# Talking-heads attention with an FNet block: raw q and k turned by VectorE in 32x32 blocks instead of by TensorE through PSUM, from the second batch on

## The chip, the cores and the metric

The kernel runs on one core of a Trainium2 chip. The metric is the device time of one execution in microseconds, the median of several runs. All data is float32.

## The reference

```python
# q, k, v: (8, 12, 448, 64)   w_pre, w_post: (12, 12)
scores = einsum("bhij,hg->bgij", (q @ k.T) / sqrt(64), w_pre)
attn   = exp(scores - max(scores, -1)); attn /= attn.sum(-1) + 1e-9
x      = (einsum("bgij,gh->bhij", attn, w_post) @ v)      # -> (8, 448, 768)
u      = x + real(fft(fft(x, axis=1), axis=2))
un     = (u - mean(u)) / sqrt(var(u) + 1e-6)
out    = u + relu(un @ w_ch1) @ w_ch2                     # 768 -> 3072 -> 768
```

The mixing of the 12 heads before and after the softmax sets the layout of the attention stage: scores of all heads must stand side by side on partitions. The weights `w_ch1` and `w_ch2` come as float64 and are converted in the kernel.

## The kernel before

The kernel has two parts: `mix_phase` (attention and Fourier mixing, to about 800 us) and `ffn_phase`. Only the first is touched.

`mix_phase` runs 184 steps, 23 for each of 8 batches (`GS` = 23, `TOT` = 184), after a prologue with negative step numbers. In step `s` these things happen, in an order that is written out by hand in `ORDERS`, one list for even steps and one for odd:

- `pre`: TensorE mixes the scores of step s+2 over heads (L656, into PSUM tiles `mx`).
- `post`: TensorE mixes the exponentials of step s over heads (L690, into `po`).
- `max0`, `max1`: VectorE takes the row maxima of step s+2 (L663). `exp0`, `exp1`: ScalarE takes the exponentials into `PP`, with their sums (L670).
- `turn`: VectorE turns `po` of step s in 32x32 blocks into `Pv` (L703).
- `scale`: VectorE makes the reciprocal of the sums of step s+2 (L677, L678), GpSimd scales `PP` with it (L680). Behind it GpSimd does one or two pieces of the Fourier folds (L785 to L806; one if a load of q or k was issued in the step).
- `QK`, `AV`: TensorE makes scores (L628) or the product with v (L720); ScalarE evicts them (L489).
- `full`: larger pieces with due steps, among them `emit_xpose`, `emit_x`, `emit_z`, `emit_s2`.
- `conv`: VectorE does one operation of the conversion of a float64 weight (`wts.deal(1)`).
- `gather`: SP gathers the scores of step s+5 into `Kr` (L645). At the start of a step, `none` issues loads of q, k and v on GpSimd's queue.

The program order of TensorE, VectorE, ScalarE and GpSimd is the order in which the pieces are emitted, so an instruction that waits holds all that stands behind it on its engine. Each step's maxima are taken two steps before its `post`.

Raw q and k of a pair of heads (`xx` = 0, 1, 2) come by `emit_load_qk`: a tile `raw` of 128 partitions, 64 for each of two groups of heads (`y`), 7 consecutive tokens on a partition, two heads side by side (`x`), by four DMAs (L572) with 64 rows of 1792 bytes in the source, written as pieces of 256 bytes. The pool `praw` has four such tiles. `emit_xpose` turns a tile by seven 128x128 transposes on TensorE (L601) into two PSUM tiles `ms`. VectorE evicts one and ScalarE the other into `qT` or `kT` (L489), four tiles of each (`pqt`). The columns of `qT` stand in the order of the tokens; the eviction writes them in steps of 7 elements:

```python
dst = _ap(t, MG + c0, [[rt, P], [1, n], [WQ, 2], [C7, 64]])       # q
dst = _ap(t, 32 * c0, [[rt, P], [32, n], [HS, 4], [1, 32]])       # k
```

The columns of `kT` may stand in any order that agrees with the rows of v, which `emit_load_v` (L581) loads.

The due steps stand in tables, counted from the first step of the batch before: `AT_T` says at which step a tile is transposed (q and k of pair 0 at 5 and 9, of pair 1 at 15 and 16, of pair 2 at 13 and 15), `AT_L` when its two halves are loaded (-8 to -1 for the first four tiles, 8 to 11 for the last two). `AT_V` gives the steps of the v loads in their own batch, `AT_QK` those of the scores. The four `qT` tiles are used in turn, so a new one needs the last score product of the batch before (block 7) that reads the old.

## Time and profile before

| what | us |
|---|---|
| median of 3 runs | 2301.55 (2299.75 to 2306.33) |
| span of the profiled execution | 2297.6 |
| TensorE (matmul) busy | 2249.2 (98%) |
| VectorE busy | 1711.2 (74%) |
| ScalarE busy | 1167.1 (51%) |
| GpSimd busy | 1292.1 (56%) |
| granted TensorE clock, mean | 0.998 |

The span runs from the first to the last instruction of one execution that was profiled; its own time is that span. The timed runs are other executions and lie 2.2 to 8.7 us above it.

How to read the rows: PE is TensorE (PEld its weight loads), DVE is VectorE, ACT is ScalarE, POOL is GpSimd, SP the queue that issues most DMAs. A group row has line, engine, operation, out<-in, partitions x elements, count, then busy time and mean ns of one, then the idle time of the engine just before these instructions and what ended it. A timeline row has start, duration, engine, line and operation, and in brackets the idle time before it with its releaser. In the busy times by stretch, each engine has its busy us and its number of instructions, and the last three columns are clock, share of the 16 DMA engines and GB/s. A row of a DMA queue has packets, MB and the share of 16 engines' time; a row of DMA issues has their count, KB of each, and the median us from issue to landing. Matmuls are pipelined and their ends are modelled, so a busy TensorE need not be one at its peak.

### The profile page before, as it was taken

To read this page: it belongs to the slowest core of one execution; us is meant where nothing else is said; L and a number is where in the kernel's file an instruction comes from. 1 tells how busy PE (TensorE), PEld (TensorE's weight loads), DVE (VectorE), ACT (ScalarE), POOL (GpSimd) and SP (SyncE) were. 2 spreads that over 40 slices of the span, in tenths; PEclk is the share of its full clock that TensorE was granted. 3 is DMA by queue.
4 is the path that set the end of the run, shared out by engine and by line. 5 is a ranking of instruction groups with operands and counts; after the bars stand their busy time and mean duration, and the time that the engine had idled before them with its cause. 6 is when DMAs were issued, how large, how long until landed. Compare 5 with 4: busy or idle time off the path is not lost.

```text
span 2297.6 us, 60793 instructions
## 1 busy us (share of the span) xinstructions
PE 2249.2 (98%) x22894; PEld 1740.7 (76%) x22894; DVE 1711.2 (74%) x3640; ACT 1167.1 (51%) x3330; POOL 1292.1 (56%) x1805
## 2 busy tenths in 40 slices
PE   7999999999999999999999999999999999999998
PEld 3455555555554677777899999999999899999998
DVE  5778787888877757776877787778778777765545
ACT  4676767767676533231445445444444445434434
POOL 7677878879768541221555555546555645454334
PEclk9999999999999999999999999999999999999999
DMA  7566565666756475649677887788787987795664
GB/s 185 168 178 181 168 192 171 190 179 181 202 151 190 143 265 182 230 162 327 191 181 180 252 214 184 212 195 242 204 197 184 277 188 174 191 257 121 143 146 76
DMA packets 228063, 439.45 MB, mean 191 GB/s; under 512 B 35964, under 2 KB 149558, under 8 KB 227772
## 3 DMA queue, kind: packets, MB, share of 16 engines
q1 hardware_dynamic: 156620, 301.52, 38.2%
q0 software_dynamic: 68864, 133.00, 30.4%
q8 instruction: 183, 3.00, 0.6%
q10 hardware_dynamic: 2288, 1.05, 0.2%
q14 instruction: 108, 0.88, 0.1%
HBM read 213.16 MB, written 143.16 MB: 155 GB/s over the span
## 4 chain that ended last, share of the span: by engine, by line
PE 87%; DVE 5%; DMA 3%; ACT 2%; issue 1%; POOL 1%; SPq 1%; ACTq 0%; DVEq 0%; POOLq 0%
PE psP L1213 18%; PE psP L1335 14%; PE psR L1213 9%; PE psR L1335 7%; PE mx L656 6%; PE ms L720 6%; PE ms L628 5%; PE po L690 5%; PE psQ L1213 4%; PE psQ L1335 3%; PE psP L1290 3%; PE ms L845 2%; PE ms L601 2%; DMA Kr<-Sb 1%; PE psR L1290 1%
## 5 line engine op out<-in xcount | busy, mean ns | idle before, releaser
L1369 POOL DMA_DIRECT2D out_dram<-od x172 | 209.1, 1276 | 261.7 <-DVE od L1357 175.3
L680 POOL TENSOR_SCALAR PP<-PP,rcp 128x448 f32<-128x448 f32 x368 | 234.6, 647 | 170.2 <-DVE rcp L678 123.8
L670 ACT ACTIVATE PP<-mx,nmx 128x448 f32<-128x448 f32 x368 | 230.2, 631 | 165.2 <-DVE nmx L663 157.2
L663 DVE TENSOR_REDUCE nmx<-mx 128x1 f32<-128x448 f32 x368 | 212.5, 618 | 101.2 <-PE mx L656 99.1
L1176 POOL TENSOR_TENSOR hq<-h 128x128 f32<-128x128 f32 (+1 forms) x210 | 130.0, 619 | 255.9 <-ACT h L1235 122.3
L1363 ACT COPY od<-psP 128x192 f32<-128x192 f32 x488 | 156.1, 320 | 172.0 <-PE psP L1335 170.6
L1366 DVE TENSOR_TENSOR od<-od 128x768 f32<-128x768 f32 x210 | 201.3, 972 | 52.7 <-ACT od L1363 52.3
L703 DVE STREAM_TRANSPOSE Pv<-po 128x896 f32<-128x896 f32 x184 | 203.7, 1107 | 2.9 <-PE po L690 2.1
L489 ACT COPY Sb<-ms 124x448 f32<-124x448 f32 (+1 forms) x378 | 181.7, 540 | 46.0 <-PE ms L628 19.2
L656 PE MATMUL mx<-Kr,kw 60*32 60x448 f32 x2944 | 192.2, 549 | 4.3 <-ACT PP L670 2.3
L628 PE MATMUL ms<-kT,qT 64*32 64x448 f32 (+1 forms) x3072 | 191.6, 545 | 3.9 <-ACT qT L489 2.8
L720 PEld LDWEIGHTS ms<-Pv,vv 64*64 64x64 f32 x5376 | 138.1, 132 | 73.7 <-issue 48.8
L690 PE MATMUL po<-PP,kw 60*32 60x448 f32 x2944 | 184.0, 537 | 1.2 <-POOL PP L680 1.1
L1213 PE MATMUL psP<-qs,w1t 128*128 128x256 f32 x744 | 179.2, 380 | 2.4 <-DVE h L1234 1.5
L1213 PE MATMUL psP<-ks,w1t 128*128 128x256 f32 x744 | 179.3, 380 | 0.4 <-DVE h L1234 0.3
L720 PE MATMUL ms<-Pv,vv 64*64 64x120 f32 (+1 forms) x5376 | 160.8, 263 | 3.6 <-ACT Sb L489 2.2
L254 POOL TENSOR_SCALAR wst<-wst 128x256 f32<-128x256 f32 (+1 forms) x76 | 118.6, 1569 | 67.2 <-ACT wst L265 66.9
L1213 PEld LDWEIGHTS psP<-qs,w1t 128*128 128x128 f32 x744 | 139.5, 190 | 19.4 <-DVE h L1234 1.9
L1213 PEld LDWEIGHTS psP<-ks,w1t 128*128 128x128 f32 x744 | 139.5, 190 | 17.2 <-DVE h L1234 0.7
L1213 PE MATMUL psP<-ub,w1t 128*128 128x256 f32 x528 | 127.2, 379 | 1.1 <-DVE h L1234 1.1
L1234 DVE TENSOR_TENSOR h<-h,psP 128x512 f32<-128x512 f32 x42 | 28.8, 686 | 127.9 <-PE psP L1213 112.3
L1335 PE MATMUL psP<-w2t,hq 128*128 128x192 f32 x490 | 122.5, 332 | 1.2 <-DVE od L1357 1.2
(199 smaller groups left out, 5301.6 us busy)
## 6 DMA issues: line engine op xcount, KB each, us to landing
Kr<-Sb SPq DMA_DIRECT2D x730, 105.0 KB
out_dram<-od POOLq DMA_DIRECT2D x172, 384.0 KB, 6.3
qs<-ub SPq DMA_DIRECT2D x89, 384.0 KB
ks<-ub SPq DMA_DIRECT2D x88, 384.0 KB
ub<-ub SPq DMA_DIRECT2D x79, 384.0 KB
w1t<-w SPq DMA_DIRECT2D x42, 384.0 KB
w2t<-w SPq DMA_DIRECT2D x42, 384.0 KB
raw<-in_moe_w_ch_dram SPq DMA_DIRECT2D x32, 384.0 KB
```

Source lines behind the costliest of these rows:

```text
L628: nc.tensor.matmul(pss[x][o:o + hi - lo, :S], st["qT", xx][64 * x:64 * x + 64, y, lo:hi], st["kT", xx][64 * x:64 * x + 64, y, :], start=Tr ...
L656: nc.tensor.matmul(mx[x][64 * z + o:64 * z + o + 32, :S], kw1[64 * x:64 * x + KR, o:o + 32], Kr[64 * x:64 * x + KR, z, :], start=True, sto ...
L663: nc.vector.tensor_reduce(nmx[:, :], steps[T]["mx"][x][:, :S], axis=AX.X, op=ALU.max, negate=True)
L670: nc.scalar.activation(steps[T]["PP"][:, x, :], steps[T]["mx"][x][:, :S], ACTF.Exp, bias=steps[T]["nmx", x][:, :], accum_out=steps[T]["den ...
L680: nc.gpsimd.tensor_scalar(PP[:, x, :], PP[:, x, :], rcp[:, x:x + 1], 1.0, op0=ALU.mult, op1=ALU.mult)
L690: nc.tensor.matmul(po[o:o + 32, z, :S], kw2[64 * z:64 * z + KR, y, :], PP[64 * z:64 * z + KR, :, c * HS:(c + 1) * HS], start=True, stop=True)
L703: nc.vector.transpose(turned[a]["Pv"][:, j, :].rearrange("p (z s) -> p z s", z=2), steps[T]["po"][:, :, :S])
L720: nc.tensor.matmul(pss[y][64 * x:64 * x + 64, :nu * R], st["v", pr][64 * y:64 * y + 64, x, jb * D:(jb + 1) * D], _ap(Pv, 64 * y * rp + 32 ...
L1213: mm = nc.tensor.matmul(p[:, m, :], w1[i][:, kc, m * P:(m + 1) * P], ub[:, kc, :], start=i in (0, 4, 1)[:3 - seed] and m == kc == 0, stop= ...
L1335: nc.tensor.matmul(ps[j, key][:, :DQ], a, b, start=m in (0, 4), stop=True, skip_group_check=True)
L1366: eng.tensor_tensor(D[j][:, :, :], D[j][:, :, :], D[k][:, :, :], op=ALU.add)
L1369: nc.gpsimd.dma_start(out=acc[t, r, d], in_=D[j][:, :, :], accum_op=ALU.add)
```

## The change

From the second batch on, `emit_load_half` and `emit_flip` take the place of `emit_load_qk` and `emit_xpose`. The first batch stays as it was.

A half load brings one group of two heads (`y`) into a whole `raw` tile by two DMAs on GpSimd's queue, one for each head. Partition 64x + 32h + j gets the tokens 14j to 14j+13 of head x, from element 32h on: 864 consecutive floats, of which every second run of 32 is used. A flip is one VectorE transpose in 32x32 blocks, 128 partitions x 14 x 32, from this tile straight into `qT` (columns in the order of the tokens, written 14 elements apart) or `kT` (runs of 32). There are twelve loads and twelve flips to a batch where there were six tiles. The two margins of `qT` are still set to zero by GpSimd.

The flips have a place of their own in `ORDERS`, behind `turn` and ahead of `scale`. Their due steps are in `AT_F` (`AT_F1` and `AT_L1` for the first pair of the second batch), counted as before from the first step of the batch before; the order of the pairs is 0, 2, 1 (`FLIP`). v is loaded in the order that fits the new columns of `kT`, by two DMAs where there was one. At the steps 12, 13 and 15 of each batch no weight conversion is done (`BARE`), and it must be finished by the end of the stage. The last score block takes pair 2 before pair 1.

```diff
-AT_L = ((-8, -7), (-6, -5), (-4, -3), (-2, -1), (8, 9), (10, 11))
+AT_L = (-8, -7, -6, -5, 7, 8, 10, 11, 13, 13, 14, 14)
+AT_F = ((0, 1, 3, 4), (12, 12, 13, 13), (14, 15, 15, 16))
+FLIP = (0, 2, 1)
 AT_V = ((2, 3), (4, 4), (5, 6))
-AT_L1 = ((-12, -12), (-12, -12), (2, 3), (4, 5), (8, 9), (10, 11))
+AT_L1 = (-12, -12, -12, -12)
+BARE = (12, 13, 15)
+AT_F1 = (3, 4, 5, 6)
...
-         (0, 1, 2), (0, 1, 2), (0, 1, 2), (0, 1, 2))
+         (0, 1, 2), (0, 1, 2), (0, 1, 2), (0, 2, 1))
...
-    "QK max1 exp1 turn scale conv full gather",
+    "QK max1 exp1 turn flip scale conv full gather",
...
-    "AV turn exp1 scale conv gather full flush"))
+    "AV turn flip exp1 scale conv gather full flush"))
...
+    def emit_load_half(b, xx, nm, y):
+
+        t = batches[b]["raw" + nm, xx, y] = praw.tile([P, C7, 2, D], F32, name="raw" + nm,
+                                                      tag="raw")
+        src = (q if nm == "q" else k)[b, 6 * y + 2 * xx]
+        for x in range(2):
+            nc.gpsimd.dma_start(
+                out=_ap(t, 64 * x * _row(t), [[_row(t), 64], [1, FR * D - 32]]),
+                in_=_ap(src, x * S * D, [[32, 2], [FR * D, 32], [1, FR * D - 32]]))
+        return True
+
+    def emit_flip(b, xx, nm, y):
...
+        t = st[nm + "T", xx]
+        rt = _row(t)
+        if nm == "q":
+            out = _ap(t, y * WQ + MG, [[rt, P], [1, FR], [FR, 32]])
+        else:
+            out = _ap(t, y * S, [[rt, P], [32, FR], [1, 32]])
+        nc.vector.transpose(out, _ap(raw, 0, [[_row(raw), P], [D, FR], [1, 32]]))
...
+        for n in range(2):
+            nc.gpsimd.dma_start(
+                out=t[:, n, :],
+                in_=_ap(v[b, h + n], 0, [[C7 * D, 2], [FR * D, 32], [1, C7 * D]]))
...
-            for at, (a, nm, xx) in zip(AT_L if b > 1 else AT_L1, sorted(at_t, key=lambda e: e[0])):
-                for y in range(2):
-                    due("none", f + at[y] - GS if b > 1 else at[y],
-                        lambda b=b, xx=xx, nm=nm, y=y: emit_load_qk(b, xx, nm, y))
-            for xx, at in enumerate(AT_T):
-                for nm, a in zip("qk", at):
-                    due("full", f + a - GS,
-                        lambda b=b, xx=xx, nm=nm: emit_xpose(b, xx, nm))
+            for i, xx in enumerate(FLIP):
+                for j, nm in enumerate("qk"):
+                    for y in range(2):
+                        n = 4 * i + 2 * j + y
+                        at, a = AT_L[n], AT_F[i][2 * j + y]
+                        if b == 1 and i == 0:
+                            at, a = AT_L1[n], AT_F1[n]
+                        due("none", f + at - GS,
+                            lambda b=b, xx=xx, nm=nm, y=y: emit_load_half(b, xx, nm, y))
+                        due("flip", f + a - GS,
+                            lambda b=b, xx=xx, nm=nm, y=y: emit_flip(b, xx, nm, y))
...
-                    if s >= 4:
+                    if s >= 4 and (s % GS not in BARE):
                         wts.deal(1)
```

`FR` is S // 32 = 14, `D` is 64, `C7` is 7, `WQ` is the width of `qT` with its margins.

27 lines of the change are left out of this document (20 added, 7 removed).

## Prediction

> **What bounds the kernel now.** I read the page's first part, then one line's count, then the busy times by stretch.
>
> ```profile
> span 2297.6 us, 60793 instructions
> ...
> PE 2249.2 (98%) x22894; PEld 1740.7 (76%) x22894; DVE 1711.2 (74%) x3640; ACT 1167.1 (51%) x3330; POOL 1292.1 (56%) x1805
> ```
>
> ```profile
> L703 DVE STREAM_TRANSPOSE Pv<-po x184: 1094/1107/1119, 39.0 to 784.9; 128x896 f32<-128x896 f32 x184
> ```
>
> The attention stage is 184 steps (8 batches of 23), each with one L703 on VectorE: (784.9-39.0)/183 = 4.08 us a step. I take the fifth batch; its step 0 begins at 413.5 us, and its step 12, the 105th L703, at 462.4.
>
> ```profile
> core 0: us, PE busy (x) PEld busy (x) DVE busy (x) ACT busy (x) POOL busy (x), PEclk, DMA share, GB/s
> 413.50:434.00 20.50, 20.18 (x428) 11.49 (x422) 16.85 (x38) 13.61 (x46) 14.40 (x21) 1.00 0.60 191
> 434.00:462.20 28.20, 27.97 (x615) 14.21 (x599) 22.99 (x47) 21.22 (x67) 27.68 (x45) 1.00 0.71 204
> 462.20:483.60 21.40, 20.71 (x402) 11.22 (x405) 17.91 (x35) 15.79 (x46) 21.08 (x35) 1.00 0.51 159
> 483.60:491.90 8.30, 8.30 (x184) 4.63 (x168) 5.81 (x13) 5.49 (x18) 5.67 (x9) 1.00 0.76 194
> ```
>
> These are steps 0-4, 5-11, 12-16 and 17-18. TensorE is busy 97 to 100% at full clock, so it sets the time. VectorE has 21.40-17.91 = 3.5 us to spare in steps 12-16, and GpSimd, whose queue is in order, is full from step 5 to 16.
>
> **What is removed.** In each of 7 batches, six groups of seven 128x128 transposes with their evictions.
>
> ```profile
> L601 PE MATMUL ms<-ident,rawq 128*128 128x128 f32 x147 | 20.6, 280 | 4.5 <-ACT Sb L489 4.5
> L601 PE MATMUL ms<-ident,rawk 128*128 128x128 f32 x147 | 20.5, 279 | 2.4 <-ACT Sb L489 2.4
> ```
>
> ```profile
> 468.34 0.99 PE L601 MATMUL ms<-ident,rawq 128*128 128x128 f32 x7 [0.53 <-ACT Sb L489]
> 469.26 0.98 PE L656 MATMUL mx<-Kr,kw 60*32 60x448 f32 x16
> ```
>
> ```profile
> L489 DVE COPY qT<-ms 128x512 f32<-128x512 f32 x21 | 23.5, 1121 | 2.6 <-PE ms L601 2.5
> ...
> L489 DVE COPY kT<-ms 128x384 f32<-128x384 f32 x21 | 11.7, 557 | 2.8 <-PE ms L601 2.8
> ```
>
> The next group starts 0.92 us after a group of seven, so six are worth 5.5 us of TensorE a batch, 39 us in all, and 1.0 us a batch of waits for PSUM go as well ((4.5+2.4)/7; I credit 0.3 outside steps 12-16). Two groups lie in steps 5-11, four in 12-16. VectorE loses 3 x 1.121 + 3 x 0.557 = 5.0 us a batch. ScalarE's six copies count nothing: it is busy 15.79 of 21.40 and its work stays beside TensorE's.
>
> **What is added on VectorE.** Twelve block transposes ("flips") of 128x448 a batch, SBUF to SBUF, which no row shows.
>
> ```profile
> L663 DVE TENSOR_REDUCE nmx<-mx 128x1 f32<-128x448 f32 x362 | 209.0, 618 | 96.3 <-PE mx L656 94.4
> ```
>
> A key flip writes runs of 32: between half of L703 (0.55 us) and 0.62, what L663 takes for 448 elements; I take 0.61. A query flip writes single elements 56 bytes apart. The old query copy writes them 28 bytes apart and takes 1121 ns for 512, against 557 for 384 in the key copy. So 0.55 to 0.98 (448/512 x 1.12); I take 0.98, the row of the same kind.
>
> Steps 12-16 get eight flips (two queries, two keys, a query, a query and a key, a key): 4 x 0.98 + 4 x 0.61 = 6.4 us. They lose two query and two key copies (3.4 us) and, by BARE, the weight conversions of steps 12, 13 and 15: three of these rows, 1.85 us.
>
> ```profile
> 463.78 0.49 DVE L289 TENSOR_SCALAR tmp<-wst 128x384 uint32<-128x384 uint32 x1
> ...
> 468.25 0.76 DVE L293 SCALAR_TENSOR_TENSOR tmp<-raw,tmp 128x384 f32<-128x384 uint32 x1
> ...
> 472.72 0.54 DVE L297 TENSOR_TENSOR wst<-wst,tmp 128x384 f32<-128x384 f32 x1
> ```
>
> (0.49 + 0.76 + 0.60 at step 15.) VectorE's work there becomes 17.9 - 3.4 - 1.85 + 6.4 = 19.0 us, where TensorE's falls to 20.7 - 3.7 = 17.0. So VectorE is the bound there, even with no wait.
>
> **The wait that is added.** The flip of step 14 is the first of the third pair, and its two loads are issued in GpSimd's step 13. All are in order: VectorE stops in front of step 14's sums and the next maxima until both have landed; ScalarE's exponentials wait for the maxima, and TensorE for the freed PSUM. How long is there? GpSimd in steps 12 and 13 of before:
>
> ```profile
> 465.73 1.24 POOL L680 TENSOR_SCALAR PP<-PP,rcp 128x448 f32<-128x448 f32 x2
> 466.94 0.99 POOL L790 TENSOR_TENSOR xs<-xs 113x383 f32<-113x383 f32 x1
> 468.00 1.45 POOL L799 TENSOR_TENSOR xq<-xs 113x191 f32<-113x191 f32 x2
> 469.41 0.18 POOL L800 COPY xq<-xs 113x1 f32<-113x1 f32 x1
> 469.57 1.25 POOL L680 TENSOR_SCALAR PP<-PP,rcp 128x448 f32<-128x448 f32 x2
> ```
>
> ```profile
> L645 POOL DMA_DIRECT2D Kr<-Sb x6: 554/576/602, 26.0 to 28.8; - x6
> ```
>
> From the start of step 12 on VectorE: L703 1.1, two flips 2.0, the reciprocals 0.3 = 3.4; then on GpSimd the scaling 1.25, the two folds 2.65, and the first of the four issues 0.58: the second load is issued at 7.9. The flip of step 14 is reached at 2 x 4.1 + 1.1 = 9.3. So 1.4 us lie between them, and the wait is the landing time less 1.4.
>
> What is the landing time? Each load is 64 rows of 3456 bytes (216 KB, of which half is not used) against 112 KB before, and its source pattern starts with a dimension of two, where the old one started with 64. The next answers are of two stretches: 4.5 to 10 us, where the loads start with 64, and 154.8 to 157.2 us, where only the gathers into Kr move, several queued, whose source starts with ten.
>
> ```profile
> q1 hardware_dynamic: 2754, 0.68, 91.3%
> ```
>
> ```profile
> q1 hardware_dynamic: 366, 0.56, 65.3%
> ```
>
> With 64 the queue keeps 91% of the sixteen engines busy; with ten and work waiting, 65%, which is 10.4 of 16. So I take it that a transfer is spread over as many engines as its first dimension lets it, and that a load that starts with two is carried by two: 108 KB (0.1106 MB) each. The DMA answer of 400 to 600 us, and one row of the whole run:
>
> ```profile
> q0 software_dynamic: 4816, 14.50, 26.3%
> ...
> rawq<-in_q_dram POOLq DMA_DIRECT2D x30, 112.0 KB, 4.3
> vv<-in_v_dram POOLq DMA_DIRECT2D x12, 224.0 KB, 4.6
> rawk<-in_k_dram POOLq DMA_DIRECT2D x24, 112.0 KB, 5.0
> ```
>
> ```profile
> Kr<-Sb POOLq DMA_DIRECT2D x6, 105.0 KB, 3.8
> ```
>
> One engine moves 14.50/(0.263 x 16 x 200) = 0.0172 MB/us here and 0.56/(0.653 x 16 x 2.4) = 0.0223 for the gathers: 6.4 or 5.0 us for a share. Beside that a landing has a fixed part: 4.3 less 0.4 for a query's 7 KB an engine is 3.9; 3.3 by Kr, 4.6 by the keys. So 8.3 to 11.0; I take 9.6, and a wait of 8.2 us (6.9 to 9.6). If all sixteen carried it, the nearest row is vv, as large: 4.6, and a wait of 3.2.
>
> [...]
>
> Steps 12-16 then take 19.0 + 8.2, less what VectorE can carry over into steps 17-18: it has 8.30-5.81 = 2.5 us there, of which I take half (0 to 2.5), since TensorE feels the delay before. That is 26.0 against 21.4: +4.6 us a batch. The loads of step 14 follow 3.4 us behind (four issues, scaling and a fold) and VectorE works as long before it needs them, so the wait comes once. The second pair is loaded about 2.3 steps (9.4 us) before its last flip: no wait at 9.6, 1.6 us at 11.
>
> **The rest.** Steps 5-11 lose two groups: -1.84, and -0.3 of PSUM waits. Steps 0-4 get four flips, 2 x 0.98 + 2 x 0.61 = 3.2 us, into 20.50-16.85 = 3.65 us of free VectorE time: +0.5 (0 to 1.5). GpSimd issues the V loads as twelve halves instead of six; here are the scalings of steps 4 and 5, and the reader of the second:
>
> ```profile
> 434.20 1.27 POOL L680 TENSOR_SCALAR PP<-PP,rcp 128x448 f32<-128x448 f32 x2
> ...
> 440.38 0.65 POOL L680 TENSOR_SCALAR PP<-PP,rcp 128x448 f32<-128x448 f32 x1
> ```
>
> ```profile
> 441.76 0.96 PE L690 MATMUL po<-PP,kw 60*32 60x448 f32 x16
> ```
>
> The second half of that scaling ends at about 441.64, 0.1 us before TensorE reads it. Three more issues come before it in steps 4 and 5, 3 x 0.52 = 1.6 us; other batches may have slack, so +0.9 (0 to 1.6). The halved V loads (3.3 us on two engines, 7.2 in all) have four steps, 16 us, and stay hidden; the issues of q and k cost 576 ns for 723, 3.5 us a batch saved on a queue that the V halves fill again. The conversions left out at three steps are made in later ones, on VectorE time that is free; without that cover they would cost 0.5 us each.
>
> Sum: 4.6 - 1.84 - 0.3 + 0.5 + 0.9 = +3.9 us a batch, x 7 = +27 us: the profile's 2297.6 becomes 2324.6. The timed runs lie 2.2 to 8.7 us above the span; on their median, 2301.55, it is **2328.5**. By one term at a time at its end (wait -1.3 or +1.4, query flips at 0.55 -1.7, carry-over +1.2, V issues +0.7, steps 0-4 +1.0), added as independent, the case spans 2308 to 2345.
>
> **Rivals.**
> 1. *No wait, faster.* GpSimd gets ahead of VectorE, and both loads of step 13 are issued some 8 us before the flip. It decides if the gap of 1.4 us is in truth 9 us or more. Then steps 12-16 are bound by VectorE's 19.0 (-2.4), and the sum is -3.1 a batch, -22 us; if VectorE overlaps better, up to TensorE's own 39 + 7 = -46. Middle: 2268. For it: TensorE is the bound everywhere else. Against: two folds and two scalings stand before those issues. Chance 0.15.
> 2. *Sixteen engines.* Wait 3.2: steps 12-16 take 19.0 + 3.2 - 1.2 = 21.0, the sum is -1.1, -8 us: 2294. Against: the 65.3%. Chance 0.12.
> 3. *TensorE alone counts.* VectorE's lag is made up in full in later steps; then 17.0 + 8.2 - 2.5 = 22.7, +1.3, sum +0.6, +4 us: 2306. Against: L656 and L663 follow each other within a step. Chance 0.10.
> 4. *The transposes were not on the path.* TensorE's 97% hides other limits, and their removal brings nothing: +3.9 + 1.84 + 0.3 = 6.0, +42 us: 2344. Against: no other engine is over 85% outside steps 5-16. Chance 0.08.
>
> [...]
>
> **How the numbers follow.** The forecast has 0.55; 0.3% is 7 us, about what a measurement can tell from no change. Slower: forecast and rival 4, and part of 3: 0.66. Same: the rest of 3, most of 2: 0.14. Faster: rival 1 and part of 2: 0.20. The range 2280 to 2346 leaves out most of rival 1 and the top.
>
> **What would show it.** Right: the flips of the third pair's first query wait on the DMA of rawq some 8 us, seven times (about 55 us of VectorE idle), landing near 9.6 us; steps 12-16 take 26 us; query flips 0.98, key flips 0.61. Wrong: landings near 4.6, no DMA wait on VectorE, steps 12-16 under 21 us, or a step-5 scaling that costs TensorE nothing.

## The result, and the profile after

The changed kernel takes 2495.11 us (median of 4 runs, 2484.16 to 2500.30) against 2301.89 for the one before: a ratio of 1.0838, 95% interval 1.0805 to 1.0870. That is 193 us slower, where the forecast was 27 (2328.5) and the range ended at 2346. The sign was right and the size was not. The profiled execution took 2500.29, and its span is below. First the page of the changed kernel, its span and busy times, then the turns of the 184 steps (count, ns min/median/max, first and last start):

```profile
span 2498.5 us, 60298 instructions
...
PE 2301.8 (92%) x22600; PEld 1746.7 (70%) x22600; DVE 1738.2 (70%) x3682; ACT 1144.7 (46%) x3288; POOL 1318.5 (53%) x1847
```

```profile
L743 DVE STREAM_TRANSPOSE Pv<-po x184: 1081/1106/1175, 50.7 to 976.7; 128x896 f32<-128x896 f32 x184
```

The span grew by 200.9 us: TensorE stood still 148.3 us more (2498.5 - 2301.8 = 196.7, against 48.4), and was "busy" 52.6 us more with fewer matmuls. The last step starts 191.8 us later than before (976.7 for 784.9): 11.7 us are lost ahead of the first step and 180 in the steps. The other 9.1 us come behind the last step. By the starts of this row and of L703 before, the eight batches together lose 97 us in steps 12-16, 55 in steps 5-11, 18 in steps 19-22, 7 in steps 0-4 and 3 in steps 17-18. The busy times by stretch of the fifth batch, steps 0-4, 5-11, 12-16, 17-18; of the batches that turn tiles for the next, it loses most in steps 12-16 and least in 5-11:

```profile
core 0: us, PE busy (x) PEld busy (x) DVE busy (x) ACT busy (x) POOL busy (x), PEclk, DMA share, GB/s
525.99:548.05 22.06, 21.73 (x454) 12.14 (x446) 20.87 (x44) 14.38 (x48) 16.27 (x25) 1.00 0.53 158
548.05:580.19 32.14, 26.47 (x572) 13.61 (x556) 20.01 (x44) 19.28 (x63) 29.15 (x45) 1.00 0.78 170
580.19:618.44 38.25, 24.95 (x380) 11.36 (x382) 18.35 (x36) 13.44 (x42) 21.13 (x36) 0.78 0.85 163
618.44:626.90 8.46, 8.46 (x180) 4.62 (x170) 5.63 (x13) 6.00 (x19) 6.60 (x10) 0.99 0.51 120
```

Steps 12-16 take 38.25 us for 21.40; the forecast was 26.0. Steps 0-11 take 54.2 for 48.7. In steps 12-16 TensorE stands still for 13.3 us, and its granted clock is 0.78, where it was 1.00 in all four stretches of before. The flips and what they wait for (us, times):

```profile
L609 DVE STREAM_TRANSPOSE qT<-rawq x42: 899/937/1000, 60.0 to 851.7; 128x448 f32<-128x448 f32 x42
L609 DVE STREAM_TRANSPOSE kT<-rawk x42: 588/603/670, 66.5 to 856.1; 128x448 f32<-128x448 f32 x42
...
  DMA rawq<-in_q_dram: 58.3, 10
  DMA rawk<-in_k_dram: 30.1, 10
```

And the landings of the loads and of the gathers into Kr:

```profile
rawq<-in_q_dram POOLq DMA_DIRECT2D x84, 216.0 KB, 12.4
rawk<-in_k_dram POOLq DMA_DIRECT2D x84, 216.0 KB, 12.6
...
vv<-in_v_dram POOLq DMA_DIRECT2D x84, 112.0 KB, 7.2
...
Kr<-Sb POOLq DMA_DIRECT2D x6, 105.0 KB, 7.8
```

What the prediction said of the flips is there: their durations, and the wait for rawq, 58.3 us where it had about 55 (though in ten waits of up to 10.0 us). But the last row says something it had not asked: a gather into Kr, whose code did not change, lands in 7.8 us for 3.8 (six of the first, which GpSimd issues behind loads on the same queue; for SP's the trace has no landing). The waits for the gathers, of the changed kernel (us in total, times, longest; ScalarE's, then SP's own queue):

```profile
ACT Sb L494 <- DMA Kr<-Sb: 91.1, 23, 9.6
```

```profile
SPq L685 <- DMA Kr<-Sb: 162.6, 118, 6.8
```

and of the kernel before:

```profile
ACT Sb L489 <- DMA Kr<-Sb: 18.6, 9, 3.7
```

```profile
SPq L645 <- DMA Kr<-Sb: 2.6, 6, 1.1
```

### The profile page after: what moved, and what is told of

Read it like the earlier page. It is cut to its first block, busy times and chain, and to the rows that moved or that the text cites. A ratio compares the mean times of both kernels' runs of the same rounds, so it can differ in the third digit from the quotient of the medians.

```text
span 2498.5 us, 60298 instructions
## 1 busy us (share of the span) xinstructions
PE 2301.8 (92%) x22600; PEld 1746.7 (70%) x22600; DVE 1738.2 (70%) x3682; ACT 1144.7 (46%) x3288; POOL 1318.5 (53%) x1847
## 5 line engine op out<-in xcount | busy, mean ns | idle before, releaser
L696 PE MATMUL mx<-Kr,kw 60*32 60x448 f32 x2944 | 239.8, 592 | 104.9 <-ACT PP L710 74.6
L703 DVE TENSOR_REDUCE nmx<-mx 128x1 f32<-128x448 f32 x368 | 213.3, 617 | 133.0 <-PE mx L696 131.1
L730 PE MATMUL po<-PP,kw 60*32 60x448 f32 x2944 | 230.1, 590 | 28.4 <-POOL PP L720 21.8
L668 PE MATMUL ms<-kT,qT 64*32 64x448 f32 (+1 forms) x3072 | 224.9, 582 | 13.3 <-ACT Sb L494 8.9
L760 PEld LDWEIGHTS ms<-Pv,vv 64*64 64x64 f32 x5376 | 144.2, 136 | 87.0 <-issue 55.3
L696 PEld LDWEIGHTS mx<-Kr,kw 60*32 60x32 f32 x2944 | 51.8, 109 | 198.6 <-ACT PP L710 117.6
L760 PE MATMUL ms<-Pv,vv 64*64 64x120 f32 (+1 forms) x5376 | 168.0, 269 | 11.7 <-issue 6.1
L730 PEld LDWEIGHTS po<-PP,kw 60*32 60x32 f32 x2944 | 69.8, 113 | 116.5 <-issue 73.5
L668 PEld LDWEIGHTS ms<-kT,qT 64*32 64x32 f32 (+2 forms) x3072 | 68.3, 112 | 95.0 <-issue 60.6
## 6 DMA issues: line engine op xcount, KB each, us to landing
rawq<-in_q_dram POOLq DMA_DIRECT2D x84, 216.0 KB, 12.4
rawk<-in_k_dram POOLq DMA_DIRECT2D x84, 216.0 KB, 12.6
```

Source lines behind the costliest of these rows:

```text
L668: nc.tensor.matmul(pss[x][o:o + hi - lo, :S], st["qT", xx][64 * x:64 * x + 64, y, lo:hi], st["kT", xx][64 * x:64 * x + 64, y, :], start=Tr ...
L696: nc.tensor.matmul(mx[x][64 * z + o:64 * z + o + 32, :S], kw1[64 * x:64 * x + KR, o:o + 32], Kr[64 * x:64 * x + KR, z, :], start=True, sto ...
L703: nc.vector.tensor_reduce(nmx[:, :], steps[T]["mx"][x][:, :S], axis=AX.X, op=ALU.max, negate=True)
L730: nc.tensor.matmul(po[o:o + 32, z, :S], kw2[64 * z:64 * z + KR, y, :], PP[64 * z:64 * z + KR, :, c * HS:(c + 1) * HS], start=True, stop=True)
L760: nc.tensor.matmul(pss[y][64 * x:64 * x + 64, :nu * R], st["v", pr][64 * y:64 * y + 64, x, jb * D:(jb + 1) * D], _ap(Pv, 64 * y * rp + 32 ...
```

## The experiments

The expectations name theories by letters that each text explains. The kernel before was run again beside each group (medians 2296.5 to 2298.6), and a ratio is against those runs. In the expectations "two engines" and "sixteen engines" stand for patterns that start with two and with 64 (or 32), after the prediction's estimate; no row counts the engines of a transfer. The first theory, that VectorE's wait for its loads is the cost, falls with e10 and e11.

**Patterns that start with 64 or 32 (e1_all64, e2_rows32).** e1 starts the patterns of q, k and v with 64. Other tokens land on each partition, so scores and outputs are of other numbers.

```diff
-                in_=_ap(src, x * S * D, [[32, 2], [FR * D, 32], [1, FR * D - 32]]))
+                in_=_ap(src, x * S * D, [[C7 * D - 8, 64], [1, FR * D - 32]]))
...
-                in_=_ap(v[b, h + n], 0, [[C7 * D, 2], [FR * D, 32], [1, C7 * D]]))
+                in_=_ap(v[b, h + n], 0, [[C7 * D, 64], [1, C7 * D]]))
```

> The changed kernel, with all loads of q, k and v from the second batch on taken by source patterns that start with 64 rows instead of two (the rows begin 440 or 448 floats apart), so other tokens and elements come into the tiles than the flips and products need: the same number of DMAs, rows, row lengths and bytes, and nothing else changes. Theory A (a load that starts with two is carried by two DMA engines, and this is what costs the time): landing of q and k falls from 12.5 us to 4.5 to 5.5, the VectorE waits for them fall from 88 us to under 25, the granted clock is back at 0.99 or more, and the time is 2294 (2280 to 2310). Theory B (VectorE's flips or the tight times of issue are the cause, whatever the landing): the time stays above 2400.

Measured: 2367.94, ratio 1.0298 (1.0281 to 1.0315). e2 keeps the tokens of the change and cuts each load into patterns of 32 rows (v alike), with 48 DMAs a batch for q and k where the change has 24:

```diff
-            nc.gpsimd.dma_start(
-                out=_ap(t, 64 * x * _row(t), [[_row(t), 64], [1, FR * D - 32]]),
-                in_=_ap(src, x * S * D, [[32, 2], [FR * D, 32], [1, FR * D - 32]]))
+            for h in range(2):
+                nc.gpsimd.dma_start(
+                    out=_ap(t, (64 * x + 32 * h) * _row(t), [[_row(t), 32], [1, FR * D - 32]]),
+                    in_=_ap(src, x * S * D + 32 * h, [[FR * D, 32], [1, FR * D - 32]]))
```

> The changed kernel with each load of q and k as two DMAs of 32 rows (one for each half of a head), four instead of two to a half load, and v by two DMAs that start with 32 rows; the tiles get exactly what they got. Theory A: 32 rows spread over 16 engines, so landings of about 4.5 to 5.5 us and a clock of 0.99, against 24 more issues of about 0.6 us on GpSimd in each batch (14 us in 95, where GpSimd had 16 free): 2300 (2280 to 2340). Theory B: above 2400.

Measured: 2390.67, 1.0397 (1.0378 to 1.0416). Two thirds of the loss, 127 us from 2495.11 to the 2367.94 of e1, go with the patterns that start with two. The rival "sixteen engines" had put the wait on them, but its 2294 is far off: 70 us stay. VectorE's waits for rawq and rawk in e1 are 20.3 and 12.4 us in all seven batches.

**Patterns that start with two in the kernel before (e3_before_two, e3c_before_64).** Here nothing is turned by VectorE; the loads of q and k of the later batches write rows of 1792 bytes, from a pattern that starts with 2, and in the control with 64 (the tokens stand in another order).

```diff
+            if b:
+                eng.dma_start(
+                    out=_ap(t, 64 * y * _row(t) + x * C7 * D, [[_row(t), 64], [1, C7 * D]]),
+                    in_=_ap(src[b, 6 * y + 2 * xx + x], 0, [[C7 * D, 2], [2 * C7 * D, 32], [1, C7 * D]]))
+                continue
```

> The kernel before, with q and k from the second batch on loaded by patterns that start with two (1792 bytes a row, 112 KB a DMA as before, contiguous in the tile; the tokens stand in another order); transposes on TensorE as before, issued at least two steps before their use. Theory A1 (two engines hurt mainly by the waits of the flips): landing about 7.5 us, which two steps cover, and the time is that of before, 2302 to 2312. Theory A2 (the gathers into Kr, which use some of the same engines, are held up as well): TensorE and ScalarE wait for Kr or its gathers, and the time is 2320 to 2360 with a lower clock.

> The control of e3_before_two: the kernel before with the same destination and the same rows of 1792 bytes, but patterns that start with 64 in place of 2 (the tokens that land on a partition are others than in before). Theory A2 (two engines in place of sixteen made the 30 us of e3_before_two): 2293 to 2305, no change from before, the landing of rawq about 4 us. If the layout of the rows made it: about 2328.

Measured: 2328.26, 1.0121 (1.0096 to 1.0147) with 2; 2293.83, 0.9981 (0.9971 to 0.9991) with 64. With 2 a load of q lands in 7.2 us, with 64 in 4.0. The waits for the gathers, with 2:

```profile
ACT Sb L489 <- DMA Kr<-Sb: 38.7, 15, 4.3
```

and with 64:

```profile
ACT Sb L489 <- DMA Kr<-Sb: 17.8, 10, 4.8
```

TensorE, which reads the tiles of q and k, waits as long for their loads in both, to half a microsecond (6.5 and 6.1 us for rawk, 0.5 and 0.5 for rawq). So the count that a pattern starts with costs 34 us here, and the waits that grew are those for the gathers.

**What a wait costs (e5_stall8, e8_stall_busy, e8b_stall_full, e8c_stall_half).** The kernel before, with eight more reductions on VectorE at step 14 of seven batches:

```diff
+                    if 0 <= s < TOT - GS and s % GS == 14:
+                        for _ in range(8):
+                            nc.vector.tensor_reduce(
+                                idle[:, :], _ap(kw1, 0, [[_row(kw1), P], [0, 14], [1, 64]]),
+                                axis=AX.X, op=ALU.max)
```

> The kernel before, with eight reductions of 128x896 (about 1 us each) added on VectorE ahead of the reciprocals of step 14 in batches one to seven: a stop of VectorE of about 8 us in seven places, with no change to any DMA. Theory C (as in the prediction, each us of the stop beyond 2 to 3 us of slack is lost once, at full clock): 5.5 us a place, 2340 (2330 to 2350), clock 0.998. Theory D (while TensorE stands still its clock is halved, and stays so for 3 to 10 us after): clock 0.5 in seven short stretches, 8 to 11 us lost a place, 2360 to 2380.

Measured: 2366.14, 1.0289 (1.0271 to 1.0306): 9.65 us a place for 8.9 us of reductions. Busy times by stretch around the first place:

```profile
97.00:102.00 5.00, 0.00 (x0) 0.00 (x0) 4.86 (x9) 0.00 (x0) 0.67 (x2) 0.71 0.35 129
102.00:107.00 5.00, 3.08 (x23) 1.80 (x31) 3.64 (x8) 3.54 (x8) 4.75 (x9) 0.50 0.20 57
107.00:112.00 5.00, 5.00 (x79) 2.00 (x71) 3.60 (x8) 2.80 (x7) 1.50 (x3) 0.77 0.34 120
```

TensorE has nothing to do for 7.8 us. Its clock is half for some 10 us, about half of them behind the stall. It looked as if each wait cost its length and then the slow matmuls (theory D). To test that, TensorE got something to do in the stall. First 96 matmuls more at the start of step 16, 64 rows by 32 columns of the array each:

```diff
+            if 16 <= s < TOT - GS + 2 and (s - 16) % GS == 0:
+                ps = ms_tile()
+                for _ in range(24):
+                    for o in range(0, 128, 32):
+                        nc.tensor.matmul(ps[o:o + 32, :448], kw1[:64, :32],
+                                         batches[s // GS]["kT", 0][:64, 0, :448],
+                                         start=True, stop=True)
```

> The kernel before with the same eight extra reductions on VectorE at step 14 of the batches 1 to 7 as in e5_stall8, and with 96 small matmuls more on TensorE, whose result nobody reads, put at the start of step 16 of the batches 0 to 6, so that TensorE has work to do that needs no scores while VectorE is held up. The output is the reference's. Theory D (a wait costs its own length and then again what TensorE loses at half clock after having stood still): if the extra matmuls fill the stall, the half clock after the seven stalls goes away, the mean granted clock stays at 0.99 or more, and the time is 2340 to 2350 us, below the 2366 of e5_stall8 although TensorE has more to do. If the loss were only the idle time itself (theory C, each microsecond of wait counted at full clock), the matmuls could at best leave it, and 2366 or more is seen. If the matmuls run at another place than the stall, they add their own 5 to 6 us a batch: 2400 us, and the run tells nothing.

Measured: 2611.34, 1.1349 (1.1312 to 1.1385): they stood behind the stall and took 35 us a batch, which tells nothing of D (but see the last section). Then matmuls of the whole array, 16 and 8, ahead of the transposes of step 15:

```diff
+            if b and xx == 1 and nm == "q" and c0 == 0:
+                for _ in range(16):
+                    nc.tensor.matmul(ps[:, :3 * P], ident[:, :], _ap(raw, 0, [[_row(raw), P], [1, 3 * P]]),
+                                     start=True, stop=True)
```

> The kernel before with the eight reductions of e5_stall8 at step 14, and 16 matmuls of 128x128 by 128x384, whose result is overwritten, put ahead of the transposes of the second pair's q at step 15, the last thing that TensorE does before it stands still for 7.8 us in e5_stall8. The output is the reference's. They take about 5 us of that stand-still at full clock and use the whole array, where those of e8_stall_busy used half of it and ran at half clock for 35 us a batch. Theory D (a wait costs its length and again what TensorE loses at half clock after it): the stand-still falls to about 3 us, the stretches at half clock behind the seven stalls go or shrink to 3.4 us, and the time is 2338 to 2352, below the 2366 of e5_stall8 with 36 us more of matmuls in it. If half clock were not what the second part of the 9.65 us a stall is made of, 2366 or more.

> e8b_stall_full with 8 of the extra matmuls in place of 16. The 16 took 10.6 us in its trace, 2.4 us more than the stand-still that they fill; 8 take 5.3 us and end before VectorE comes back. Theory D (half clock after the stand-still is a part of what a stall costs): the clock stays full and the 2.4 to 3.4 us a stall of matmuls at half clock go: 2342 to 2350 us, with more work on TensorE than in the 2366 of e5_stall8. If half clock costs nothing, because VectorE's backlog sets the pace behind the stall anyway: 2362 to 2370.

Measured: 2366.61, 1.0292 (1.0274 to 1.0309) with 16; 2364.90, 1.0291 (1.0267 to 1.0314) with 8. The same places with 16, where the clock stays full:

```profile
99.00:104.00 5.00, 5.00 (x17) 3.01 (x16) 4.86 (x8) 0.00 (x0) 0.55 (x1) 1.00 0.35 129
104.00:109.00 5.00, 5.00 (x25) 3.36 (x24) 2.88 (x7) 2.55 (x7) 4.87 (x10) 1.00 0.18 51
```

The mean clock of the run is 0.982 in e5, 0.991 with 8 and 0.997 with 16 matmuls, and the three times lie within 2 us, where theory D had 2338 to 2352. That does not yet make theory D fall. What half clock adds to the matmuls is TensorE's busy time, less the extra matmuls, above the 2249.2 of before: 14.5 us in e5 (2263.7), 12.1 with 8 (2299.3 - 38.0) and nothing with 16 (2319.2 - 74.1). With 8, TensorE still stands still, for 2.47 us at the place shown in the last section, and sixteen matmuls behind it take 1.79 us for 0.96, so almost nothing was taken away; most of the time at half clock that went had been stand-still. With 16 all was taken away, but they ended 2.4 us late at seven places, 17 us, about what the full clock saved. So a stall of 8.9 us on VectorE costs 9.65, about its own length, and whether the longer matmuls behind it are a part of that stays open, as it does for the 52.6 us of longer matmuls in the changed kernel.

**Moving issues and turns (e6_v_sp, e7_late, g2_pairs).** In all three the patterns start with 64 or, in g2, with 32. e6 issues the v loads of e1 on SP's queue:

```diff
-            nc.gpsimd.dma_start(
+            nc.sync.dma_start(
                 out=t[:, n, :],
```

> The changed kernel with its loads of q, k and v from patterns that start with 64 (as in e1_all64: other tokens land on each partition, so the output is another), and the loads of v of the batches after the first issued on SP's queue in place of GpSimd's. Theory V: the idle of TensorE at steps 5 and 6 (2.9 us a batch in e1_all64, where AV waited for scales of GpSimd) comes from the issues of the v loads on GpSimd, 2 each of about 0.7 us a half; without them those waits go and half a stretch of half clock behind them: 2335 to 2350 us against the 2368 of e1_all64. Theory W: the scales are late because GpSimd works at its limit there for other reasons (its gathers and its additions), and the time stays at 2360 to 2370. SP's own waiting issues could also hold the v loads up: AV would then wait for DMA vv by name, and the time is above 2370.

e7 puts the flips of the third pair one step later in e1:

```diff
-AT_F = ((0, 1, 3, 4), (12, 12, 13, 13), (14, 15, 15, 16))
+AT_F = ((0, 1, 3, 4), (12, 12, 13, 13), (15, 16, 16, 17))
-BARE = (12, 13, 15)
+BARE = (12, 13, 16)
-AT_QK = ((0, 2, 1), (0, 1, 2), (0, 1, 2), (1, 2, 2),
+AT_QK = ((0, 3, 2), (0, 1, 2), (0, 1, 2), (1, 2, 2),
```

> e1_all64 (other tokens, the output is another) with the turns of the third pair one step later (steps 15, 16, 16, 17 in place of 14, 15, 15, 16) and the first matmuls of the scores that use it moved behind them. Theory T: what is left of the waits at steps 14 and 15 in e1_all64 (VectorE waits 1.0 to 5.8 us for rawq at step 14 and 1.2 to 3.4 for rawk at step 15, 20.3 + 12.4 us in the sum of both rows) is only that the loads are issued too shortly ahead of the turns; a step of 4 us more takes most of both away, TensorE's idle at steps 13 to 15 of 4.5 us a batch falls to 1 to 2, and with the half clock behind it the time is 2325 to 2345 us. Theory B: the buffers of raw come free one step later too, so the loads move with the turns and the same wait stands at the next step: 2360 to 2375.

g2 computes what the change computes, with four DMAs of 32 rows for both halves of a pair, v on SP and later flips:

```diff
-AT_L = (-8, -7, -6, -5, 7, 8, 10, 11, 13, 13, 14, 14)
-AT_F = ((0, 1, 3, 4), (12, 12, 13, 13), (14, 15, 15, 16))
+AT_L = ((-6, -5), (7, 9), (14, 15))
+AT_F = ((1, 5, 6, 7), (12, 13, 13, 14), (16, 16, 17, 17))
...
+                    in_=_ap(src, x * S * D + 32 * h,
+                            [[FR * D, 32], [6 * S * D, 2], [1, FR * D - 32]]))
```

> The same computation as the changed kernel, its output the reference's. VectorE turns q and k as in the change, but one load brings both halves of a pair in 4 DMAs whose patterns start with 32 (24 DMAs a batch for q and k, where e2_rows32 has 48), the v loads start with 32 too and are on SP's queue, and the turns stand one to three steps later than in the change. If the loss of the change was two engines for the loads (theory A), the tight distance from load to turn (T) and the issues on GpSimd (V) together, this version should have none of the three: 2270 to 2310 us, about the time of before. If a wait of VectorE is left anywhere in each batch, each costs its length and as much again at half clock: 2320 to 2370.

Measured: 2372.04, 1.0316 (1.0286 to 1.0345); 2390.07, 1.0391 (1.0361 to 1.0422); 2412.93, 1.0500 (1.0471 to 1.0529). None gained: e6 lies 2 us above theory W's range, e7 and g2 above all that was expected. g2 also has half as many tiles, each twice as large. e7 is the one that told: VectorE's waits fell by two thirds, and the run became 22 us slower. Waits of e7_late:

```profile
ACT Sb L494 <- DMA Kr<-Sb: 75.2, 18, 9.2
...
DVE kT L609 <- DMA rawk<-in_k_dram: 8.5, 7, 2.4
...
DVE qT L609 <- DMA rawq<-in_q_dram: 3.5, 4, 1.8
```

The wait of 32.7 us for loads became 12.0, and ScalarE's wait for gathers rose from 58.4 to 75.2. Removing a wait did not remove time: something else was late behind it. (The scores that read the third pair also moved a step, so this alone is no proof.)

**Loads without readers (e10_noload, e11_unread, e11b_unread64, e12_qk_two, e13_v_two, e14_half64).** In these the flips read a tile of 240 floats a partition that is loaded once, at the same steps and with the same outputs' layout, so the scores are of other numbers and no instruction waits for a load of q or k. What differs is which loads still run beside it.

```diff
+        if not batches[0].get("held"):
+            batches[0]["held"] = True
+            nc.gpsimd.dma_start(out=_ap(held, 0, [[_row(held), P], [1, 240]]),
+                                in_=_ap(q, 0, [[FR * D, P], [1, 240]]))
+        return True
...
-        nc.vector.transpose(out, _ap(raw, 0, [[_row(raw), P], [D, FR], [1, 32]]))
+        nc.vector.transpose(out, _ap(held, 0, [[_row(held), P], [16, FR], [1, 32]]))
```

This is e10, with v as in e1. In the four with loads the `return True` is left out; e11 has the patterns of the change, e11b those of e1, e12 patterns that start with two for q and k alone, e14 rows half as long. e13 is e10 with v as in the change.

> The changed kernel without any load of q and k after the first batch: the turns read a small tile that is loaded once (the scores of the later batches are those of other numbers), at the same steps and with the same output layout; v is loaded by patterns that start with 64. What is left is the change without its transfers: TensorE's transposes gone, VectorE turning at the new steps. The prediction's own sum without the wait of 8.2 us gives 3.9 - 8.2 = -4.3 us a batch, 2270 us. Theory A (all of the loss is data that come late, for q and k or for the gathers beside them): 2255 to 2285. Theory F (VectorE's turns, put where they are, delay the scores' chain and let TensorE stand still whatever the loads do): above 2295, with TensorE standing still at steps 12 to 15 although no wait for a load exists.

> The changed kernel with all of its loads, q, k and v, from patterns that start with 2 as in the change, but with the turns reading the small tile of e10_noload (the scores are of other numbers): no instruction waits for a load of q or k any more, while their traffic stays on the two engines. After minus this run is what VectorE's waits for the loads cost; this run minus e10_noload is what the traffic costs by way of the gathers into Kr, the v halves and the buffers. Theory W (the waits at steps 14 and 15 with the half clock behind them are nearly all of it): at most 30 us above e10_noload, so 2270 to 2310. Theory G (traffic that shares the two engines holds the gathers up, as the 30 us of e3_before_two showed for the kernel before): 50 to 100 us above e10_noload, with ACT Sb waiting 70 us or more for DMA Kr.

> e11_unread with the patterns of e1_all64: the changed kernel with all loads of q, k and v starting with 64, the same 216 KB each, and the turns reading the small tile (other numbers). No instruction waits for a load of q or k. Theory E (two engines in place of sixteen are what holds the gathers up): 2296 to 2310, close to e10_noload, and the 70 us that e1_all64 lost are VectorE's waits for its loads. Theory Y (twice the bytes hold the gathers up on sixteen engines too): 2340 to 2370, as e1_all64, with ACT Sb waiting 50 us or more for DMA Kr.

> e11_unread with the v loads starting with 64: only q and k are loaded by two engines, and nothing waits for them (other numbers in the scores and in v). If q and k make the loss, 24 of the 36 small loads of a batch and four fifths of the bytes: 2440 to 2485. If the v halves, which land beside the gathers of steps 2 to 7, make half of it: 2380 to 2420.

> e10_noload with the v loads of the change, whose patterns start with 2; q and k are not loaded. The complement of e12_qk_two: if two engines for v cost little by themselves, 2296 to 2312; if they make half of the loss, 2370 or more.

> e11b_unread64 with rows of 1728 bytes in place of 3456: 64 rows a load, sixteen engines, the same 24 loads of q and k a batch at the same steps, nobody waits for them (other numbers in the scores). Theory Y (the bytes): half of them, about those of before, and 2297 to 2315, with ACT Sb waiting 20 to 35 us for DMA Kr. Theory P (the places: eight half loads in the steps 7 to 14, ahead of the scores of steps 15 to 19, where before had four): 2350 to 2377, as with the whole rows.

Measured, as a ladder; each step adds one thing (ratio differences times 2298):

| run | what runs beside the flips | median us | ratio (95%) | step us |
|---|---|---|---|---|
| e10_noload | no loads of q, k | 2296.71 | 0.9994 (0.9983-1.0006) | |
| e14_half64 | 24 loads a batch, 108 KB, patterns that start with 64 | 2327.96 | 1.0139 (1.0112-1.0165) | +33 |
| e11b_unread64 | the same with 216 KB | 2376.57 | 1.0340 (1.0312-1.0368) | +46 |
| e12_qk_two | the same, q and k by patterns that start with 2 | 2475.72 | 1.0773 (1.0757-1.0788) | +100 |
| e11_unread | v by patterns that start with 2 too | 2485.25 | 1.0802 (1.0778-1.0826) | +7 |
| the change | flips read what was loaded | 2495.11 | 1.0838 (1.0805-1.0870) | +8 |

The last two steps are within the intervals; v by patterns that start with two, by itself (e13_v_two, 2312.84, 1.0065 from 1.0051 to 1.0079) costs 16 us above e10. The traffic makes the loss, and VectorE's waits for it, the wait of the prediction, make 8 of 193 us or none: in e11 VectorE waits for no load, and the same time is lost elsewhere. The pair with 64 says the same: with the reader (e1_all64) 1.0298, without it (e11b_unread64) 1.0340. Against what was expected, e10 lies in theory F's range but not for its reason (its steps 12-16 are shorter than before, see below), e11 lost nearly twice what theory G allowed, e14 lies between its two theories, and e11b, e12 and e13 lie in or just above a range they had been given. Where the time goes, shows the timeline of ScalarE in the fifth batch of e11_unread:

```profile
601.11 0.62 ACT L715 ACTIVATE PP<-mx,nmx 128x448 f32<-128x448 f32 x1
601.63 0.20 ACT L715 ACTIVATION_READ_ACCUMULATOR PP<-mx,nmx 128x1 f32 x1
608.42 0.97 ACT L494 COPY Sb<-ms 124x448 f32<-124x448 f32 x2 [6.59 <-DMA Kr<-Sb]
609.27 0.65 ACT L715 ACTIVATE PP<-mx,nmx 128x448 f32<-128x448 f32 x1
```

The score tiles `Sb` are two (`psb`). ScalarE may not write the next block until the gathers out of the old one have landed; the exponentials of the next step stand behind this copy, and TensorE behind them. The chain of work that ended last goes through the gathers for 11% of the span in e11, and for 1% in the kernel before. Over the run ScalarE's wait is 144.4 us in e11, 117.9 in e12, 84.8 in e11b, 16.4 in e10:

```profile
ACT Sb L494 <- DMA Kr<-Sb: 144.4, 26, 10.2
```

```profile
ACT Sb L494 <- DMA Kr<-Sb: 84.8, 23, 9.9
```

```profile
ACT Sb L494 <- DMA Kr<-Sb: 16.4, 8, 5.9
```

From e11b to e12, the step of 100 us, GpSimd's scalings are not what grows: matmuls wait 26.0 us for them after 25.6. What it is in these patterns was not separated: besides landing later, the loads that start with two leave about twice as many packets under 512 bytes in the trace (74284 for 36652 in e12), for the same bytes. And the six gathers that GpSimd issues land in 8.3 us in both, so it is SP's gathers, by the rows below, that tell the two apart.

In e14, the first step of the ladder, ScalarE's wait for the gathers is as short as in e10 (15.9). There GpSimd is late: the waits of e14_half64 for its scalings, and of e10_noload:

```profile
PEld po L735 <- POOL PP L725: 61.8, 51, 5.5
...
PE po L735 <- POOL PP L725: 33.6, 26, 4.7
```

```profile
PEld po L736 <- POOL PP L726: 34.7, 39, 3.6
...
PE po L736 <- POOL PP L726: 17.4, 14, 2.8
```

These +43.3 us of waits (of weight loads and of matmuls, which can overlap) stand beside the +33 us of time; sixteen of the 24 issues of a batch stand in steps 7 to 14, each ahead of the scaling of its step, where the kernel before has eight. That the issues do it, and not the traffic of the 108 KB loads, is argued from these rows.

**The change with its loads mended (g3s).** Only the bytes that are used, 32 rows first, tiles half as large and loaded earlier; the output is the reference's.

```diff
-AT_L = (-8, -7, -6, -5, 7, 8, 10, 11, 13, 13, 14, 14)
+AT_L = (-10, -9, -8, -7, -6, -5, -4, -3, 7, 8, 10, 11)
...
+        for c in range(2):
+            for y in range(2):
+                nc.gpsimd.dma_start(
+                    out=_ap(t, (64 * x + 32 * c) * _row(t) + y * FR * 32,
+                            [[_row(t), 32], [32, FR], [1, 32]]),
+                    in_=_ap(src, 32 * c + y * 6 * S * D, [[FR * D, 32], [D, FR], [1, 32]]))
```

> The same computation as the change, its output the reference's, with loads that bring only the bytes that are used: pieces of 128 bytes, 14 for each of 32 rows, patterns that start with 32, 48 DMAs a batch of 56 KB for q and k, the tiles half as large so that the loads can stand 7 to 12 steps ahead of their turns; v by patterns that start with 32, two DMAs a half as in the change. Theory Y: no delay of the gathers beyond that of before, 2300 to 2330, the bound of e10_noload and what 24 issues more on GpSimd cost (576 ns each, 14 us a batch on an engine that is half idle). If pieces of 128 bytes hold the engines as long as the rows of 3456 bytes did, or the issues hold GpSimd's scalings up: 2340 to 2380.

Measured: 2376.81, 1.0345 (1.0314 to 1.0377). The gathers are on time again, and GpSimd, with 48 issues a batch, is not:

```profile
PEld po L735 <- POOL PP L725: 94.1, 64, 3.7
...
PE po L735 <- POOL PP L725: 43.9, 40, 2.9
...
ACT Sb L494 <- DMA Kr<-Sb: 20.7, 9, 4.5
```

Both of the kernel's tight places show here: fewer bytes cost more issues. No version was found that beats the kernel before, and e10 says why one by this way would be hard: even with q and k for nothing this version only draws level. Some 8 us of that are a wait for a late weight (below), which other places for the conversions might remove; that was not tried.

## Why the prediction was right and wrong, step by step

**The step that failed** is "What is the landing time?" and what was done with it. The prediction saw that a load is twice as large, took it to be carried by two engines, and charged this to the reader of the load alone. To the gathers into Kr, which it had quoted at 65.3% of the sixteen engines' time, it charged nothing. That zero is the 146 us of the ladder's two middle steps. SP's wait for the gathers, with patterns that start with 64 (e11b_unread64) and with two (e12_qk_two), the same bytes:

```profile
SPq L690 <- DMA Kr<-Sb: 69.6, 61, 2.4
```

```profile
SPq L690 <- DMA Kr<-Sb: 154.3, 103, 7.0
```

So SP waits 2.2 times as long for its gathers beside the loads that land later. By what means was not shown: which engines carried what is in no row here.

**The landing itself:** 12.6 us (8.9 to 19.5) for 9.6 (8.3 to 11.0). The pattern that starts with two does land later, as the prediction took it: 12.5 us for rawq in e12, 6.5 in e11b with 64, for the same bytes. The terms of the prediction's 9.6 (two engines, 6.4 or 5.0 us for a share, 3.3 to 4.6 us fixed) were estimates from rows of before; no run shows the terms, only the landings. Nothing in the sum slowed the loads by the gathers.

**The wait of 8.2 us, once a batch:** the waits are there, 58.3 + 30.1 = 88.4 us, 12.6 a batch, with a second wait for the keys that "the wait comes once" had excluded. (The keys' loads were put 3.4 us behind the queries'; the four issues, the scaling and the fold named there add up to about 4.5.) Their price was the mistake. The stalls of e5 cost about their length (9.65 us for 8.9), so the prediction's way of pricing a wait is sound where everything else is on time; here something else was late by as much, and without the waits (e11) 8 us are won at most.

**Steps 12-16:** 38.25 us for a forecast of 26.0 in the batch shown. The part without the wait can be tested alone, in e10_noload, steps 0-4, 5-11 and 12-16:

```profile
398.49:420.48 21.99, 21.49 (x454) 11.93 (x446) 20.24 (x44) 14.41 (x48) 16.30 (x27) 1.00 0.56 166
420.48:449.59 29.11, 26.04 (x580) 12.54 (x568) 19.73 (x44) 19.39 (x63) 24.00 (x38) 1.00 0.55 167
449.59:468.24 18.65, 18.17 (x378) 9.47 (x378) 17.46 (x36) 13.32 (x42) 11.45 (x22) 1.00 0.30 111
```

18.65 us stands against the 19.0 of the sum: VectorE's work there was counted rightly. Over the run e10 is 20.7 us shorter in steps 12-16 than the kernel before, where the sum had seven times 2.4. The prices of the flips were right as well, 603 ns for 0.61 and 937 for 0.98, the latter by the row of the old query copy.

**Steps 0-11:** here the sum had -1.84 - 0.3 + 0.5 + 0.9 = -0.7 us a batch; e10 has 51.1 for 48.7 in the fifth batch, and 11.8 us more over all eight, 8.2 of them in steps 5-11. So the gain of two transposes in steps 5-11 did not come. The term that was too small is the V issues on GpSimd, +0.9: this is the wait for the scalings quoted above for e10_noload, 34.7 us of weight loads and 17.4 of matmuls (2.3 more a batch for the matmuls), where the kernel before has:

```profile
PEld po L690 <- POOL PP L680: 12.1, 33, 1.2
```

```profile
PE po L690 <- POOL PP L680: 1.1, 4, 0.4
```

e6_v_sp took the v issues off GpSimd, and its wait of matmuls for scalings fell from the 20.0 us of e1_all64 to 1.4. Its time did not fall, and what took the gain back is open.

**The conversions left out,** "made in later ones, on VectorE time that is free", were another term at nothing. In the kernel before the last converted weight of the stage is sent to memory at 720.7 us (`w<-wst`, L243), long before its end; in the change at 996.0, 19 us after the last step begins. ScalarE and, behind it, TensorE wait for that store once, where the second part begins:

```profile
1002.88 0.58 ACT L1268 COPY h<-psP 128x512 f32<-128x512 f32 x1 [12.18 <-DMA w<-wst]
```

```profile
1003.90 1.62 PE L804 MATMUL ms<-ident,XT 128*113 128x128 f32 x6 [7.91 <-ACT X L494]
```

TensorE's 7.9 us are most of the 9.1 us lost behind the last step. ScalarE's wait (11.8 to 13.3 us) is in every run that is built on the change, e10 too, and in none that is built on the kernel before. That is why e10, whose last step starts 12.1 us earlier than before (772.8), ends only 3.6 us earlier, though TensorE is busy 23.3 us less (2225.9). No run puts the conversions back, so this price is read from the traces alone.

**The issues of q and k, "3.5 us a batch saved":** a saving in GpSimd's busy time, not in its place. An issue took 684 ns, not 576, and sixteen of 24 stand in steps 7 to 14, where GpSimd was full (27.68 us busy of 28.20 in steps 5-11 before). e14 minus e10 puts the loads' 24 issues, with half their bytes, at 33 us, 4.8 a batch, for nothing in the sum (168 issues more over the run, with GpSimd busy 1282.5 us for 1195.8, 0.52 us each).

**The rivals.** "No wait, faster" (2268): without any wait for loads the time is that of before (e10) at best. "Sixteen engines" (2294): the patterns that start with two do cost most, 127 us, and the time without them is still 2368 (e1). "TensorE alone counts" (2306): a lag of VectorE is not made up, as e5 shows with 9.65 us lost for 8.9. "Transposes not on the path" (2344): in e10 the gain comes in steps 12-16 and not in steps 5-11, so it is half right, and no part of the loss. None of them had the gathers in it.

## What to carry to other kernels

When a change makes a transfer larger or later to land (here 216 KB for 112, and 12.4 us for 4.3), charge it to every other transfer that runs beside it first, and look for the one with the least slack; here it was the gather that frees one of two buffers, and the wait row of the engine that refills the buffer (18.6 us before) named it. A wait that shows in the trace is not yet a price: leave the reader out and keep the traffic, or keep the reader and leave the traffic out, before mending the wait. And count issues by the steps in which they stand, not by their sum: the 24 a batch of e14 went with 33 us, where the prediction had a saving.

## What the runs showed of the hardware

At the first place of e5_stall8, a stand-still of 7.8 us, TensorE's granted clock was half from about 3.0 us after the last matmul before it (which ended at 96.1) to about 5.4 us after the start of the first behind it (103.9), by the stretches above. In e8c_stall_half a stand-still of 2.47 us was enough for slower matmuls, sixteen in 1.79 us for 0.96:

```profile
197.69 0.96 PE L695 MATMUL po<-PP,kw 60*32 60x448 f32 x16
...
207.99 0.98 PE L606 MATMUL ms<-ident,rawk 128*128 128x128 f32 x7 [2.47 <-ACT Sb L489]
208.90 1.44 PE L661 MATMUL mx<-Kr,kw 60*32 60x448 f32 x16
210.05 1.79 PE L695 MATMUL po<-PP,kw 60*32 60x448 f32 x16
```

In e8_stall_busy, matmuls of 64 rows by 32 columns ran without a pause for 35.32 us and the clock stayed at half:

```profile
110.00:115.00 5.00, 5.00 (x32) 1.19 (x28) 0.00 (x0) 0.00 (x0) 0.00 (x0) 0.50 0.01 5
...
135.00:140.00 5.00, 5.00 (x32) 1.35 (x28) 0.00 (x0) 0.00 (x0) 0.00 (x0) 0.50 0.00 0
140.00:145.00 5.00, 5.00 (x56) 1.75 (x56) 0.29 (x1) 0.00 (x0) 0.00 (x0) 0.60 0.02 3
145.00:150.00 5.00, 4.97 (x84) 1.83 (x67) 4.96 (x10) 3.97 (x12) 2.58 (x4) 1.00 0.23 86
```

It was full again, 1.00 in the next 5 us, when the kernel's own matmuls had come back (at 142.0). Beside the matmuls of e8b_stall_full, which fill the whole array, it was 1.00 in both stretches of the stall. So here a TensorE that the profile showed busy for 5.00 of 5.00 us had its clock at 0.50 in one run and at 1.00 in another; whether the rows, the columns or the pauses between such matmuls count was not tried.
